# Memory attention woven with a Mixer MLP: when the Mixer's first and last layers may take weight buffers, what margin the planner gives their loads, and which queue carries the final prefetch

## The chip, the cores and the metric

One core of a Trainium2 chip runs the whole kernel as one static program. The metric is device time in microseconds (us), the median of several runs. The mean granted TensorE clock lay between 0.984 and 0.991 of full speed in all of them. The kernel before takes about 3534 us.

## The reference

Two kinds of layer alternate on 2048 tokens of width 640: A, B, A, B, each with its LayerNorm and residual.

```python
# A: recurrent memory attention; 64 segments of 32 tokens, 8 memory tokens carried along
for s in range(n_seg):
    h = jnp.concatenate([mem, xs], axis=1)          # 40 rows
    q, k, v = h @ Wq, h @ Wk, h @ Wv                # 32 heads of 192
    ...                                             # masked softmax, p @ v
    o = jnp.einsum('bhte,hed->btd', o, Wo)
    mem = o[:, :M, :]                               # the next segment needs this
# B: Mixer MLP
h = gelu(layernorm(x) @ w1)
hs = shifted(h) @ w2                                # four quarters, shifted by -1, +1, -2, +2 tokens
x1 = x + hs
return x1 + gelu(layernorm(x1) @ w3) @ w4
```

The recurrence through `mem` forces one attention step after another. The kernel runs the second A layer five steps behind the first, so that 69 steps handle both ("two lanes", 80 columns). A step needs all of Wq, Wk, Wv and Wo. The kernel keeps about three fifths of them on the chip (3 of 5 blocks of each head group's Wq, Wk and Wv); the rest, 48 blocks of Wq, Wk and Wv and 18 of Wo, is streamed again in each step.

## The kernel before

Every instruction is first described to a planner as an operation with an engine, a duration, a due time and the buffers that it touches. A list scheduler then places them: on each engine it takes, among those that can start at once, the one with the earliest due time. What it places is the order of the program. All it believes of transfers are these constants.

```python
HG = 4                       # heads in a group: 8 head groups in a step
RING = 16; RING_A = 14; RING_B = 5    # weight buffers; attention's and Mixer's caps
STEP = 48.0; HOLD = 4.0
W1 = (0.15, 0.04); W2 = (0.4, 0.04); W3 = (0.75, 0.055); W4 = (1.5, 0.025)   # due: first, per block, in steps
LAT = 0.2; DMA_RATE = 345.0e3; DMA_LAT = 2.2; DMA_SKEW = 2.0; FLIGHT = 10
```

```python
    # in Plan.place, when operation o is placed
    if o.dma:
        srv = max(s + DMA_LAT, srv) + o.dma / DMA_RATE
        done = srv + DMA_SKEW
    ...
    for b in o.slots:
        b.left -= 1
        b.free_at = max(b.free_at, done + LAT)      # buffer free again
    ...
    for x in o.succ:
        if o.dma:
            at = done                               # user may start
```

Attention's loads ("ra" buffers) go out from SyncE, Mixer's ("rb") from GpSimd. Each queue is sorted by due time and stays in that order. A load is issued as soon as its buffer is free, however early that is; nothing else holds it back, but for a limit of ten transfers in flight on SyncE (`FLIGHT`). Which buffer a load gets is fixed by the plan.

```python
    def load_b(c, nm, n, due):
        if c >= NCH - 2:
            return ahead[nm, n]                     # last two chunks: prefetched
        b = ring("rb")
        ...
        add("POOL", POOL_US, due, fn, w=(b,), dma=P * wd * 2, queue="wb")

    # attention: the loads of Wo of all eight head groups (held is true for each of them) are due
    # in the last 4 us of the step, those of the last head group's Wv along with its matmuls
    at = base + STEP - HOLD + 0.5 * g if held else s0 + 1.9 * sl
    ws = [block(t, "o", g, c, at + 0.03 * c) for c in range(GC)]

    # last Mixer layer
    def chunk_end(c):
        ...
        for n in range(FC):                         # 12 blocks
            due = D(W4[0] + W4[1] * n)
            wb, wv = load_b(c, "w4", n, due)
            ...                                     # two matmuls of 320 columns: "y"

    # main loop: a chunk per pair of steps
    for t in range(T_A):
        c = (t - 2) // 2 if t >= 2 and t % 2 == 0 else None
        mixer = chunk(c) if c is not None else iter(())
        next(mixer, None)
        attention_step(t)
        for _ in mixer: pass
        if c is not None:
            chunk_end(c)
```

When the weights that stay resident have been used for the last time, `prefetch` loads the 32 weight blocks of the last two chunks into their tiles, from GpSimd (a chunk has w1 5, w2 5, w3 10 and w4 12 blocks).

## Time and profile before

| | before |
|---|---|
| time, median of 3 runs | 3533.37 us (3530.52 to 3536.09) |
| TensorE (PE) busy | 96% of the span |
| PE's stalls over full pace in 28 pairs of steps | 88.5 us |
| DMA | 308 GB/s mean |

Full pace means columns / 2.4 GHz + 2.5 ns for each matmul; the prediction derives it. A stall is a distance between two starts that exceeds this by over 20 ns. The second measure that I use throughout is a place in time: a pair of steps holds 16 head groups, numbered 0 to 15, and "12.05" is 5% into group 12. Groups 7 and 15 end a step, and so does the hand-over of `mem` to the next one.

The same stretch as a window of the profile: the columns are its length, then each engine's busy time and number of instructions, the granted clock, the DMA share and GB/s.

```profile
350.00:3200.00 2850.00, 2797.93 (x69832) 2737.28 (x69829) 2029.09 (x5929) 1456.10 (x2962) 735.56 (x1306) 1.00 0.95 311
```

The first pair after the length is PE. In a kernel whose PE is always busy, the number of matmuls done in a fixed stretch is a better sign of speed than the busy time: 69832 here.

The names in the lines that follow: psk, psq and psv are PE's matmuls for K, Q and V, psy those of attention's output projection (with Wo), y those of the Mixer's last layer (with w4). `wst` is a buffer of the ring, and what follows its arrow is the weight that was loaded into it.

### The profile page before, as it was taken

How to read it: one execution, taken by the hardware profiler on the slowest of the kernel's cores; microseconds unless marked ns; L12 is line 12 of the kernel's file. 1: busy time of each engine (PE TensorE's matmuls, PEld its weight loads, DVE VectorE, ACT ScalarE, POOL GpSimd, SP SyncE). 2: the span in 40 equal slices, each digit the busy share in tenths (PEclk: the TensorE clock that was granted, in tenths of full speed). 3: DMA queues.
4: the chain of work that ended last, by engine and by line, in shares of the span. 5: the costliest groups of instructions: out<-in, count | busy, mean ns of one | idle time of the engine just before them, and what ended most of it. 6: DMA issues, size and time to landing. Idle time of an engine off the chain costs nothing.

```text
span 3534.4 us, 194661 instructions
## 1 busy us (share of the span) xinstructions
PE 3384.3 (96%) x84693; PEld 3257.0 (92%) x84693; DVE 2378.1 (67%) x7184; ACT 1714.3 (49%) x3583; POOL 883.9 (25%) x1581
## 2 busy tenths in 40 slices
PE   6899999999999999999999999999999999999897
PEld 4789999999999999999999999999999999999786
DVE  2456777777666777676677776766667777766455
ACT  2334555545554555454445554545455554554343
POOL 1022222222222222222222222222222222222222
PEclk9999999999999999999999999999999999999898
DMA  9999999999999999999999999999999999999995
GB/s 339 308 304 312 311 314 311 312 309 316 311 314 310 312 309 307 315 304 311 301 314 310 306 315 309 308 305 313 308 310 324 310 313 308 313 309 313 298 317 193
DMA packets 735258, 1089.24 MB, mean 308 GB/s; under 512 B 95358, under 2 KB 691596, under 8 KB 734400
## 3 DMA queue, kind: packets, MB, share of 16 engines
q1 hardware_dynamic: 669504, 874.19, 75.5%
q0 software_dynamic: 64896, 202.59, 17.1%
q8 instruction: 662, 10.85, 1.3%
q14 instruction: 196, 1.61, 0.1%
HBM read 1071.16 MB, written 5.24 MB: 305 GB/s over the span
## 4 chain that ended last, share of the span: by engine, by line
PE 80%; DMA 14%; issue 4%; DVE 1%; POOL 1%; ACT 0%; SPq 0%; POOLq 0%; DVEq 0%; ACTq 0%
PE psy L653 15%; PE psq L514 14%; PE psv L555 14%; PE psk L514 14%; DMA wst<-in_B_w_dram 5%; PE psvt L567 5%; PE pss L586 4%; PE pso L634 4%; PE psh L1025 3%; DMA wst<-in_A_Wv_dram 3%; DMA wst<-in_A_Wo_dram 2%; PE y L1047 2%; PE pst L619 2%; PE hs L994 1%; PE psh L968 1%
## 5 line engine op out<-in xcount | busy, mean ns | idle before, releaser
L472 POOL DMA_DIRECT2D wst<-in_B_w_dram x1056 | 581.7, 551 | 1690.5 <-PE psy L653 387.9
L640 DVE CAST oT<-pso 128x480 bf16<-128x480 f32 (+1 forms) x552 | 342.3, 620 | 413.6 <-PE pso L634 412.6
L571 ACT COPY V<-psvt 80x768 bf16<-80x768 bf16 (+1 forms) x552 | 439.3, 796 | 332.1 <-PE psvt L567 323.5
L514 PEld LDWEIGHTS <-wst 128*128 128x128 bf16 x13248 | 555.6, 100 | 31.2 <-issue 10.2
L653 PE MATMUL psy<-oT,wo 128*128 128x80 bf16 (+1 forms) x10350 | 511.0, 199 | 21.1 <-DMA wo<-in_A_Wo_dram 9.1
L522 ACT CAST qT<-psq 128x480 bf16<-128x480 f32 (+1 forms) x552 | 292.5, 530 | 441.7 <-PE psq L514 364.2
L555 PE MATMUL psv<-hT,wv 128*128 128x80 bf16 (+1 forms) x9936 | 477.8, 199 | 6.2 <-issue 3.5
L514 PE MATMUL psk<-hT,wk 128*128 128x80 bf16 (+1 forms) x9936 | 465.0, 199 | 5.6 <-issue 4.2
L514 PE MATMUL psq<-hT,wq 128*128 128x80 bf16 (+1 forms) x9936 | 454.7, 199 | 12.4 <-DMA wq<-in_A_Wq_dram 7.1
L561 ACT CAST vTs<-psv 128x480 bf16<-128x480 f32 (+1 forms) x552 | 292.1, 529 | 335.0 <-PE psv L555 325.0
L653 PEld LDWEIGHTS <-wo 128*128 128x128 bf16 x10350 | 423.0, 99 | 28.3 <-issue 12.5
L597 DVE CUSTOM_DVE_ANT_1 pss<-pss,mask 80x320 f32<-80x320 f32 (+1 forms) x512 | 245.8, 480 | 270.3 <-PE pss L586 228.5
L555 PEld LDWEIGHTS <-wv 128*128 128x128 bf16 x9936 | 405.3, 99 | 20.2 <-issue 4.3
L514 PEld LDWEIGHTS <-wk 128*128 128x128 bf16 x9936 | 399.7, 100 | 14.4 <-issue 6.5
L514 PEld LDWEIGHTS <-wq 128*128 128x128 bf16 x9936 | 393.6, 100 | 20.8 <-DMA wq<-in_A_Wq_dram 8.1
L514 PE MATMUL psk<-hT,wst 128*128 128x80 bf16 (+1 forms) x6624 | 352.9, 199 | 8.6 <-issue 8.0
L653 PE MATMUL psy<-oT,wst 128*128 128x80 bf16 (+1 forms) x6210 | 351.8, 199 | 8.8 <-DMA wst<-in_A_Wo_dram 4.7
L555 PE MATMUL psv<-hT,wst 128*128 128x80 bf16 (+1 forms) x6624 | 342.6, 199 | 12.4 <-DMA wst<-in_A_Wv_dram 9.2
L624 ACT COPY PT<-pst 80x320 bf16<-80x320 bf16 (+1 forms) x552 | 223.0, 404 | 261.6 <-PE pst L619 258.8
L514 PE MATMUL psq<-hT,wst 128*128 128x80 bf16 (+1 forms) x6624 | 326.2, 199 | 8.3 <-DMA wst<-in_A_Wq_dram 5.2
L604 ACT ACTIVATE pss<-pss,sm 80x320 f32<-80x320 f32 (+1 forms) x552 | 261.4, 474 | 137.4 <-DVE sm L597 137.3
L609 DVE TENSOR_REDUCE sm<-pss 80x4 f32<-80x320 f32 (+1 forms) x552 | 251.9, 456 | 92.5 <-ACT pss L604 91.7
(135 smaller groups left out, 5501.6 us busy)
## 6 DMA issues: line engine op xcount, KB each, us to landing
wst<-in_A_Wk_dram SPq DMA_DIRECT2D x1104, 192.0 KB, 4.7
wst<-in_A_Wq_dram SPq DMA_DIRECT2D x1104, 192.0 KB, 4.7
wst<-in_A_Wv_dram SPq DMA_DIRECT2D x1104, 192.0 KB, 4.8
wst<-in_A_Wo_dram SPq DMA_DIRECT2D x1242, 160.0 KB, 4.7
wst<-in_B_w_dram POOLq DMA_DIRECT2D x726, 160.0 KB, 5.0
wst<-in_B_w_dram POOLq DMA_DIRECT2D x330, 192.0 KB, 5.3
wk<-in_A_Wk_dram SPq DMA_DIRECT2D x8, 576.0 KB, 7.6
wq<-in_A_Wq_dram SPq DMA_DIRECT2D x8, 576.0 KB, 7.4
```

The costliest lines, as they stand in the source:

```text
L472: return (nc.sync if B_SP else nc.gpsimd).dma_start(out=T(b)[:, 0:wd], in_=src)
L514: nc.tensor.matmul(out=o[:, c, 0:N], lhsT=w[:, c * P:(c + 1) * P], rhs=h[:, kc, c0:c0 + N], start=pq.begin(), stop=True, skip_group_check= ...
L522: nc.scalar.copy(out=q[:, :, 0:N], in_=T(pq)[:, :, 0:N])
L555: nc.tensor.matmul(out=o[:, c, 0:N], lhsT=w[:, c * P:(c + 1) * P], rhs=h[:, kc, c0:c0 + N], start=pv.begin(), stop=True, skip_group_check= ...
L561: nc.scalar.copy(out=vs[:, :, 0:N], in_=T(pv)[:, :, 0:N])
L571: nc.scalar.copy(out=V_[0:N, :, 0:Dh], in_=T(pt)[0:N].rearrange("n c f -> n (c f)").rearrange("n (i e) -> n i e", i=HG))
L597: nc.vector.tensor_tensor_reduce(out=o, in0=o, in1=maskt.unsqueeze(1).to_broadcast([N, HG, N]), scale=-scale, scalar=3.0e38, op0=ALU.add, ...
L604: nc.scalar.activation(out=o, in_=o, func=ACT.Exp, bias=sm_[0:N, 0:1], scale=-1.0)
L609: nc.vector.reduce_sum(out=sm_[0:N, 4:4 + HG], in_=o, axis=AX.X)
L624: nc.scalar.copy(out=Pt[0:N, :, 0:N], in_=T(pst)[0:N, :, 0:N])
L640: nc.vector.tensor_copy(out=o_[:, :, 0:N], in_=T(pso)[:, :, 0:N])
L653: nc.tensor.matmul(out=T(psy[j])[:, m - m0, c0:c0 + N], lhsT=w[:, m * P:(m + 1) * P], rhs=o_[:, c, 0:N], start=psy[j].begin(), stop=True, ...
```

## The change

The intent is to leave more of the 16 buffers to attention: the Mixer's weights should sit in them only shortly before use.

1. w1 waits until the last head group of the step before its chunk begins.
2. The twelve w4 blocks wait, four at a time, for head groups 2, 3 and 4 of the chunk's second step (10, 11 and 12 of the pair). For that the description of `chunk_end` moves behind the second step's attention.
3. The planner counts a GpSimd load as ready 1.5 us later, and a Mixer buffer as free 0.5 us after its last use, not 0.2.
4. The final prefetch goes through SyncE's queue, sorted with attention's loads, 8 us later.

The waits of 1 and 2 exist in the plan alone. The planner places such a load after the marked matmul, but no semaphore goes with it; on the chip GpSimd goes on as soon as the former user of the block's buffer is done.

```diff
+B_SLACK = 1.5
+AH = 8.0
+B_FREE = 0.5
...
-                b.free_at = max(b.free_at, done + LAT)
+                b.free_at = max(b.free_at, done + (B_FREE if b.cls == "rb" else LAT))
...
-                    at = done
+                    at = done + (B_SLACK if o.e == "POOL" else 0.0)
...
-    def load_b(c, nm, n, due):
+    def load_b(c, nm, n, due, after=()):
...
+                mark[t, g] = now[:1]          # first Q matmul of head group g of step t
...
-                return nc.gpsimd.dma_start(out=tl[:, i % 3, 0:wd], in_=src)
-            add("POOL", POOL_US, base + at * 0.6 * STEP, fn, ..., queue="wb")
+                return nc.sync.dma_start(out=tl[:, i % 3, 0:wd], in_=src)
+            add("SP", SP_US, base + at * 0.6 * STEP + AH, fn, ..., queue="wa")
...
-            wb, wv = load_b(c, "w1", kc, due)
+            wb, wv = load_b(c, "w1", kc, due, mark.get((2 * c + 1, NG - 1), ()))
...
-            wb, wv = load_b(c, "w4", n, due)
+            wb, wv = load_b(c, "w4", n, due, mark.get((2 * c + 3, 2 + n // 4), ()))
...
-        if c is not None:
-            chunk_end(c)
+        if t >= 3 and t % 2 == 1:
+            chunk_end((t - 3) // 2)
```

(Comments are mine, and long lines are cut at "...".)

More of the change, by code (lines that the diff above doesn't have):

```diff
@@ L472, in fn @@
             return (nc.sync if B_SP else nc.gpsimd).dma_start(out=T(b)[:, 0:wd], in_=src)
-        add("SP" if B_SP else "POOL", SP_US if B_SP else POOL_US, due, fn, w=(b,), dma=P * wd * 2, queue="wb")
+        add("SP" if B_SP else "POOL", SP_US if B_SP else POOL_US, due, fn, w=(b,), dma=P * wd * 2, queue="wb", after=after)
         return b, lambda: T(b)[:, 0:wd]
@@ L485 @@
     last = [()]
+    mark = {}
     def HX(t, kc):
@@ L848, in fn @@
             def fn(op, tl=tl, i=i, wd=wd, src=src):
-                return nc.gpsimd.dma_start(out=tl[:, i % 3, 0:wd], in_=src)
-            add("POOL", POOL_US, base + at * 0.6 * STEP, fn, w=(ub,), a=(b,), dma=P * wd * 2, queue="wb")
+                return nc.sync.dma_start(out=tl[:, i % 3, 0:wd], in_=src)
+            add("SP", SP_US, base + at * 0.6 * STEP + AH, fn, w=(ub,), a=(b,), dma=P * wd * 2, queue="wa")
             ahead[nm, n] = ub, lambda tl=tl, i=i, wd=wd: tl[:, i % 3, 0:wd]
@@ L1123 @@
             pass
-        if c is not None:
-            chunk_end(c)
-    for c in range((T_A - 2 + 1) // 2, NCH):
-        for _ in chunk(c):
-            pass
-        chunk_end(c)
+        if t >= 3 and t % 2 == 1:
+            chunk_end((t - 3) // 2)
+    chunk_end(NCH - 2)
+    for _ in chunk(NCH - 1):
+        pass
+    chunk_end(NCH - 1)
     placed = plan.place()
```

## The prediction

> **What bounds the kernel now.** The kernel is one static order of instructions that a planner inside it lays out. 69 attention steps (8 head groups each) stream their weights through a ring of 16 buffers; a Mixer chunk is woven into each pair of steps, and its 32 weight blocks (w1: 5, w2: 5, w3: 10, w4: 12) go through the same ring, at most 5 buffers at a time, issued by GpSimd. I read the page first: engine shares, slices, queues.
>
> ```profile
> PE 3384.3 (96%) x84693; PEld 3257.0 (92%) x84693; DVE 2378.1 (67%) x7184; ACT 1714.3 (49%) x3583; POOL 883.9 (25%) x1581
> ...
> PE   6899999999999999999999999999999999999897
> ...
> GB/s 339 308 304 312 311 314 311 312 309 316 311 314 310 312 309 307 315 304 311 301 314 310 306 315 309 308 305 313 308 310 324 310 313 308 313 309 313 298 317 193
> ```
>
> TensorE is nearly full from 350 to 3200 us, DMA moves about 311 GB/s all along. A 96% busy PE may still hide slack, so I took the distance between starts of matmuls from the trace. In one piece of the timeline 18 K/Q/V matmuls of 80 columns take 0.81 us, the last one modelled as 0.20: 0.61 / 17 = 36 ns each, which is 80 / 2.4 GHz + 2.5 ns. If every matmul between 350 and 3200 us took only columns (at least 64) / 2.4 GHz + 2.5 ns, they would need 2747 of the 2850 us. So the middle of the run is PE-bound to 96.4%, and the most that any better ordering of loads can win there is 103 us. Of the 103, I counted gaps of over 20 ns by what ended them: 42 us nothing that the profile shows ("issue"), 35 us a weight DMA, 12 us VectorE; the rest is spread thinly.
>
> Then the waits of PE:
>
> ```profile
> engine line waited for: us in total, times, longest us
> PE y L1047 <- DMA wst<-in_B_w_dram: 14.6, 23, 1.9
> PE psv L739 <- DVE vb L731: 13.8, 7, 3.9
> PE psk L514 <- issue: 12.2, 14, 2.4
> ...
> PE psv L555 <- DMA wst<-in_A_Wv_dram: 9.2, 13, 2.3
> ...
> PE psq L514 <- DMA wst<-in_A_Wq_dram: 5.2, 6, 1.3
> PE psy L653 <- DMA wst<-in_A_Wo_dram: 4.7, 10, 1.1
> ```
>
> The largest single wait is "y", the Mixer's last layer, for its own weights w4. To place the stalls I numbered the head groups of a pair of steps 0 to 15 (28 pairs, steps 8 to 63, 100.1 us each) and summed PE's excess by group: group 7 28 us, groups 13 and 14 together 22.5 us (of which y on w4 20.9), group 15 15 us, everything else 23 us. So the w4 stall costs 0.75 us per chunk.
>
> Last, why w4 is late, from GpSimd's timeline around one chunk:
>
> ```profile
> 1020.23 1.19 POOL L472 DMA_DIRECT2D wst<-in_B_w_dram  x2 [1.23 <-DMA wst<-in_A_Wq_dram]
> 1022.00 0.55 POOL L472 DMA_DIRECT2D wst<-in_B_w_dram  x1 [0.58 <-PE y L1047]
> 1024.58 0.55 POOL L472 DMA_DIRECT2D wst<-in_B_w_dram  x1 [2.03 <-PE psq L514]
> ...
> 1028.61 0.60 POOL L472 DMA_DIRECT2D wst<-in_B_w_dram  x1 [1.40 <-PE psv L555]
> ...
> 1053.46 0.59 POOL L472 DMA_DIRECT2D wst<-in_B_w_dram  x1 [3.54 <-PE pss L586]
> ```
>
> These first five are w1 of the next chunk; its first matmul starts at 1052.71, so five of sixteen buffers are taken for 26 to 32 us. Over all chunks the medians are: w1 is issued in groups 14.0 to 15.3 and used in group 2.7 of the next pair. w4 blocks 0 to 4 are issued in groups 8.0 to 10.1 and wait 5 to 11 us landed; blocks 5 to 11 must wait for those buffers, are issued from 12.05 on, fly about 5 us, and reach PE 0.0 to 0.8 us ahead of use, in each case with some chunks at zero. The planner believes that they come in time; they do not. All Mixer blocks together hold 446 buffer-us per pair, 28% of the ring's 1600.
>
> **What the Trainium skill says.** "TensorE: Matmul & The Clock Gate", section "Wait — 56ns, not 53.3ns?", gives N / 2.4 GHz + about 2.5 ns for warm back-to-back matmuls; the 36 ns above agrees, and my floor rests on it. "Perfetto Trace Analysis", "Identifying the Most-Contended Engine", warns that matmul busy share does not show the distance to the roofline; here it said 98% in the middle where the floor says 96.4%, so both leave little. "DMA: Bandwidth & Descriptors", "Issuing engines are not separate DMA queues": loads from different engines share the same 16 DMA engines, so moving the final prefetch from GpSimd to SyncE should buy no bandwidth, only an order. The trace can't quite confirm it: the fastest stretch of the end, 3465 to 3470 us, ran at 376 GB/s with both queues active.
>
> **The change, part by part.** No byte, matmul or vector instruction is added or removed; only order, waits and buffers.
>
> (1) w1 waits for the first Q matmul of group 7 of the step before its chunk (15.0 on my scale). Medians were 13.97, 14.13, 14.46, 15.00, 15.25, so three blocks move by about 1.1, 0.9 and 0.6 groups. At some 4.5 us a group: 12 buffer-us freed per pair. w1 stays over 20 us early, so nothing is risked.
>
> (2) w4 blocks 0-3, 4-7, 8-11 wait for groups 10, 11, 12 of the pair. Blocks 0 to 4 move from 8.0, 9.1, 9.4, 9.7, 10.1 to 10.2 (11.2 for block 4), some 25 buffer-us. Blocks 5 to 11 are issued after 12.05 already, so the marks do not bind them. Together with (1) 37 buffer-us, 37 / (1600 - 446) = 3% more ring for attention, all in groups 8 to 11 and 13 to 15.
>
> (3) The planner now takes a GpSimd load as ready 1.5 us later and a Mixer buffer as free 0.5 us (not 0.2) after use. w4 landed 0 to 0.8 us ahead at the median and the longest wait was 1.9; with 1.5 us more nearly all those waits vanish, since PE has K/Q/V work of later groups to put in between. I take 85% of 0.75 us x 34 chunks = 25.5: 22 us.
>
> (4) Attention's weight waits on PE between 350 and 3200 us are what remains of the 35 us after y's 20.9: 14 us. More ring in groups 13 to 15, where a third of them are (group 15 had 4.2 on Wo and 1.6 on Wv), saves perhaps 5 us.
>
> (5) The first and last five steps have one lane, thus matmuls of 40 columns; there PE is about 91% busy by the modelled ends and the loads set the pace at 301 to 315 GB/s. 3% more ring there is worth at most 3% of some 450 us; since up to ten transfers are in flight whatever the ring holds, I take a quarter to a third, 4 us.
>
> (6) The last chunks' 32 blocks now go by SyncE in one queue with step 68's weights, 8 us later. Before, GpSimd threw them in between and three times PE stood still for 0.8 to 2.3 us on Wv and Wq. But all the same bytes must land before the second-last chunk's y, and then the last chunk's chain follows (from 3504 to 3534 us, unchanged). 0 to 5 us; I take 2.
>
> Sum: 22 + 5 + 4 + 2 = 33 us. 3533 - 33 = 3500.
>
> **Rivals.** (a) The wait only moves: w4 pushed against its use by the marks makes all twelve blocks just-in-time, where five were safe. For: a 5 us flight, and a mark at 10.2 that lands block 0 at about 11.3, where its use was at 11.5. Against: the 1.5 us margin is known to the planner, which then uses y later, and y has no deadline before group 16. If it holds, the y stall stays and the time is within 0.3%: 3525 to 3540. (b) PE is bound by things that loads do not touch: 42 us "issue", 12 us VectorE. That is certain and caps the gain at about 103 us for a perfect order; it makes over 2% (71 us) unlikely. (c) The freed ring does more than I give it: DMA reached 340 to 354 GB/s in groups 9 and 10, where the ring refills, against 296 to 310 in groups 7, 13 to 15. If attention runs further ahead, part of group 7's 28 us and group 15's 15 us goes too: 3465 to 3480. (d) One ordered queue for the end makes SyncE the bottleneck or lets w4 arrive after attention is done: 5 to 10 us lost at the end.
>
> **Range and chances.** Any change of the plan shuffles the whole static order; I allow 10 us for it either way on top of (a) and (c). Range 3468 to 3527. Over 2% faster needs 3463: nearly all weight waits and half of "issue" gone, 9%. Over 2% slower needs 71 us of new stalls, and the marks leave slack everywhere but at w4: 2%.
>
> **What would show it.** Right: PE's wait "y for wst from B_w" falls from 14.6 to under 4 us; w1's issue bunches after the start of group 7; between 350 and 3200 us the work that was done there takes about 25 us less; the final chain from psx to the output store still takes 30 us. Wrong: y's wait is as large as before or comes back as attention waiting for Wk, Wq, Wv (rival a); "issue" grows as the loads run denser; the last step lengthens beyond its 59 us.

## The result and the profile after

| | before | after |
|---|---|---|
| median of 4 runs | 3534.73 us (3530.52 to 3537.48) | 3549.91 us (3542.94 to 3554.97) |
| ratio of the means | | 1.0043, 95% interval 1.0021 to 1.0064 |
| needed at full pace by the matmuls between 350 and 3200 us | 2747 us | 2738 us |
| stalls of PE in 28 pairs | 88.5 us | 93.7 us |

A ratio is the mean time of one kernel's fast runs over that of the other's of the same rounds, so it is not quite the ratio of the medians that stand beside it. The change made the kernel 0.4% slower, where 0.9% faster was predicted; 3549.91 lies above the range of 3468 to 3527.

The page of the changed kernel, engine shares and slices:

```profile
PE 3393.7 (96%) x84693; PEld 3263.4 (92%) x84693; DVE 2366.3 (67%) x7184; ACT 1716.2 (48%) x3583; POOL 840.6 (24%) x1549
...
GB/s 339 316 308 302 309 306 311 306 307 311 308 312 312 309 306 315 295 314 313 309 309 307 295 302 317 309 315 315 313 315 306 317 310 316 309 316 317 306 297 172
```

Nothing in these lines tells which kernel is slower: the same matmuls, the same 96%, the same rate. The window from 350 to 3200 us tells it:

```profile
350.00:3200.00 2850.00, 2793.11 (x69574) 2733.13 (x69572) 2013.89 (x5917) 1455.01 (x2954) 711.57 (x1304) 1.00 0.95 310
```

PE issued 258 matmuls fewer than before in the same 2850 us. PE's waits, with the same columns as in the prediction:

```profile
PE psv L560 <- DMA wst<-in_A_Wv_dram: 27.7, 39, 2.1
PE psv L744 <- DVE vb L736: 13.0, 5, 4.3
PE psy L658 <- DMA wst<-in_A_Wo_dram: 9.9, 21, 1.9
...
PE y L1052 <- DMA wk<-in_B_w_dram: 1.7, 2, 1.0
```

The wait of y for w4 in the ring, the largest before, is gone from the list altogether; what y still waits for, 2.0 us in all, are blocks of the final prefetch (`wk` and `wv` are resident tiles that it fills). In place of the old wait PE waits 27.7 us, not 9.2, for streamed blocks of Wv, and 9.9, not 4.7, for streamed Wo. The sum of those two grew by 23.7 us, more than the 14.6 that went.

GpSimd's timeline around the last layer of one chunk (the one just before the w1 loads that the prediction's timeline shows):

```profile
1007.91 0.54 POOL L475 DMA_DIRECT2D wst<-in_B_w_dram  x1 [21.54 <-DMA wst<-in_A_Wq_dram]
1008.99 0.54 POOL L475 DMA_DIRECT2D wst<-in_B_w_dram  x1 [0.54 <-PE psq L518]
...
1014.54 0.56 POOL L475 DMA_DIRECT2D wst<-in_B_w_dram  x1 [2.09 <-PE psv L560]
1016.39 0.54 POOL L475 DMA_DIRECT2D wst<-in_B_w_dram  x1 [1.29 <-PE y L1052]
...
1033.23 0.54 POOL L475 DMA_DIRECT2D wst<-in_B_w_dram  x1 [5.12 <-DMA wst<-in_A_Wo_dram]
```

GpSimd stands for 21.5 us, until head group 10, and issues w4 blocks 0 and 1. Block 2 goes out 5.6 us after block 1: in between GpSimd issues small loads for the next chunk (cut here), then it waits 2.1 us for a matmul with Wv, the last user of the buffer that the plan has given to block 2. Counted from issue to last use, 10 to 12 of the 16 buffers are attention's at that time and 2 the Mixer's, so some stand empty. The last line is the first block of the next chunk's w1, at 15.21 on the scale of groups; before it was at 13.97, the 1020.23 of the prediction's lines (at this point the trace of the changed kernel is 7 us behind). Over 28 pairs the median issue of w4 moved from 8.01, 9.09, 9.42, 9.71, 10.12, 12.05 ... 13.67 to 10.45, 10.74, 12.04, 12.24, 12.41, 12.74 ... 14.30, and the last y from 14.80 to 15.25.

The time that the change adds to the run can be split along the trace, with a caution that follows. In the two profiled runs, of 3534.4 and 3551.0 us, the second-last attention step starts 4.0 us later, lasts 6.0 us longer (45.9 and 51.9), the last step and the chain to the output store add 0.2, and from the issue of the last store to the end of the program it takes 6.4 us longer (3.5 and 9.8). The 4.0 is the sum of 1.2 us before step 8, 5.6 us in the 28 pairs (100.34 instead of 100.14 us each) and 2.9 us won back in steps 64 to 66. The caution: one profile is one execution. The changed kernel, the one with the old prefetch and the one with half of it (both below) run the same instructions on PE in the same order up to step 64; their profiles reach that step 4.5 and 11.8 us apart from the changed kernel's, with stalls of 93.7, 91.3 and 88.3 us. So of this split only the last part is firm; it comes back in every run with the new prefetch. GpSimd's last line of before and of after, in the timeline (start, length, what it does):

```profile
3530.95 0.58 POOL L1065 DMA_DIRECT2D out_dram<-xo  x1 [11.36 <-DVE xo L1053]
```

```profile
3541.17 0.56 POOL L1070 DMA_DIRECT2D out_dram<-xo  x1 [11.36 <-DVE xo L1058]
```

The store lands 1.8 us after its issue in both. Along with its issue starts a DRAIN of GpSimd, an instruction of the kernel's end that the timeline does not list; the program's last instructions wait for it. The trace records 2.72 us for it before and 9.07 after.

### The profile page after: what moved, and what is told of

It reads as the page before. It is cut to its first block, busy times and chain, and to the rows that moved or that the text cites. A ratio compares the mean times of both kernels' runs of the same rounds, so it can differ in the third digit from the quotient of the medians.

```text
span 3551.0 us, 194390 instructions
## 1 busy us (share of the span) xinstructions
PE 3393.7 (96%) x84693; PEld 3263.4 (92%) x84693; DVE 2366.3 (67%) x7184; ACT 1716.2 (48%) x3583; POOL 840.6 (24%) x1549
## 5 line engine op out<-in xcount | busy, mean ns | idle before, releaser
L475 POOL DMA_DIRECT2D wst<-in_B_w_dram x1056 | 572.9, 543 | 2148.1 <-DMA wst<-in_A_Wq_dram 431.6
L658 PE MATMUL psy<-oT,wo 128*128 128x80 bf16 (+1 forms) x10350 | 520.3, 199 | 15.2 <-DMA wo<-in_A_Wo_dram 7.8
L518 PE MATMUL psk<-hT,wk 128*128 128x80 bf16 (+1 forms) x9936 | 491.0, 199 | 7.4 <-issue 5.5
L518 PEld LDWEIGHTS <-wk 128*128 128x128 bf16 x9936 | 413.6, 100 | 18.3 <-issue 7.4
L560 PE MATMUL psv<-hT,wst 128*128 128x80 bf16 (+1 forms) x6624 | 352.1, 199 | 29.7 <-DMA wst<-in_A_Wv_dram 27.7
L518 PE MATMUL psq<-hT,wst 128*128 128x80 bf16 (+1 forms) x6624 | 343.3, 199 | 9.4 <-DMA wst<-in_A_Wq_dram 4.2
L535 DVE CAST kT<-psk 128x320 bf16<-128x320 f32 (+1 forms) x552 | 253.6, 459 | 102.5 <-PE psk L518 102.0
```

Of the source, the lines that this page charges most:

```text
L475: return (nc.sync if B_SP else nc.gpsimd).dma_start(out=T(b)[:, 0:wd], in_=src)
L518: nc.tensor.matmul(out=o[:, c, 0:N], lhsT=w[:, c * P:(c + 1) * P], rhs=h[:, kc, c0:c0 + N], start=pq.begin(), stop=True, skip_group_check= ...
L535: nc.vector.tensor_copy(out=k4[:, :, 0::3, 0:N], in_=p4[:, :, 0::2, 0:N])
L560: nc.tensor.matmul(out=o[:, c, 0:N], lhsT=w[:, c * P:(c + 1) * P], rhs=h[:, kc, c0:c0 + N], start=pv.begin(), stop=True, skip_group_check= ...
L658: nc.tensor.matmul(out=T(psy[j])[:, m - m0, c0:c0 + N], lhsT=w[:, m * P:(m + 1) * P], rhs=o_[:, c, 0:N], start=psy[j].begin(), stop=True, ...
```

## The experiments

First I had four theories, by the four parts. A: w1's blocks, held back to group 15, bunch there and collide with the loads at the step's end. B: w4 is too late, and its loads crowd out attention's. C: the margins only move PE's wait from w4 to attention's weights. D: the loss lies in the end of the program, from the new prefetch. Each of the first four kernels is the changed kernel with one part undone. (All four undone give the order of before, instruction by instruction.) Unless a run says otherwise, "measured" is the median of six fast runs, with the ratio to the kernel before of the same rounds on the same chip and its 95% interval; a point is a hundredth of that ratio, 35 us; the "middle" is 350 to 3200 us of the profiled run.

**w1's wait undone.**

```diff
-load_b(c, "w1", kc, due, mark.get((2 * c + 1, NG - 1), ()))
+load_b(c, "w1", kc, due)
```

> The changed kernel with the wait of w1 alone taken out. Theory A (bunching): the wait lets all five w1 loads go together in group 15 (issued at 15.2 to 15.7), in the middle of the stream of Wo and Wv, and this delays Wv of group 15 (18.0 us of waits in 28 pairs) and Wk and Wq of group 0 (7.8 us). Then without it PE's wait for streamed Wv falls from 27.7 us to about 10, and the time from about 3548 to about 3527. Theory B (late w4): the wait of w4 is to blame, and here the Wv wait stays above 20 us and the time at 3543 to 3553. Theory D (the end): the same as B, and the last two steps stay as they are.

Measured: 3547.68 us, 1.0039 (1.0018 to 1.0060), the same as the changed kernel. A falls. The stalls of group 15 even rose, from 23.4 to 43.7 us in 28 pairs, 19.2 of them waits of Wo's matmuls for attention's own output `oT` from VectorE, while groups 0 and 7 lost less. Here w4 blocks 2 and 3 go out at 11.05 and 11.31 (12.04 and 12.24 in the changed kernel) and block 11 at 13.90 (14.30), and the time is the same. So the slow order has more than one form, and the wait for Wv is only one of them.

**w4's wait undone.**

```diff
-load_b(c, "w4", n, due, mark.get((2 * c + 3, 2 + n // 4), ()))
+load_b(c, "w4", n, due)
```

> The changed kernel with the wait of w4 alone taken out. Theory B (late w4): the wait gives w4's buffers to attention, w4 gets them back only after group 12, the last y falls to group 15.25 and the buffers that w1 needs come free late, so all runs together in group 15. Then without it the last y is back at about 14.8, PE's wait for streamed Wv falls from 27.7 to about 10 us, and the time to about 3527. Theory A (bunching of w1): Wv waits stay above 20 us, time 3543 to 3553. In both the y wait stays under 4 us, if the margin is what removed it; if the wait of w4 removed it, it is back at some 15 us.

Measured: 3506.92 us, 0.9924 (0.9903 to 0.9944). This one wait costs 1.19 points against the changed kernel, 42 us. B is right as to the part. The waits of PE:

```profile
PE psv L560 <- DMA wst<-in_A_Wv_dram: 17.5, 19, 2.4
...
PE y L1052 <- DMA wst<-in_B_w_dram: 0.7, 2, 0.4
```

y still hardly waits, and PE did more:

```profile
350.00:3200.00 2850.00, 2810.91 (x70392) 2756.07 (x70389) 2041.87 (x5981) 1471.53 (x2988) 734.26 (x1317) 1.00 0.95 313
```

That is 818 matmuls more than the changed kernel and 560 more than before. Stalls in 28 pairs fell from 93.7 to 62.5 us. The last y is at 15.13, hardly earlier than 15.25 and not back at 14.8 as B expected, so a late y alone is not the explanation. Nor did the wait for Wv fall to 10 us: by what ended them, the 31 us of stalls that w4's wait adds in 28 pairs are 13 us for Wv, 5 for Wq and Wk and 10 for which the profile shows no cause ("issue").

**The margins undone.**

```diff
-B_SLACK = 1.5
+B_SLACK = 0.0
-B_FREE = 0.5
+B_FREE = 0.2
```

> The changed kernel with the margins set back (0 and 0.2 us instead of 1.5 and 0.5). If the margin is what removed the waits of y for w4, they are back, at 14 us or more (with the wait of w4 all twelve blocks come just in time, so up to 25 us). Theory C (the margins only move the wait on: PE takes attention work in y's place and runs into weights that are not there): the wait for streamed Wv falls from 27.7 to about 12 us and the sum of both stays within 8 us of now, time within 6 us of the changed kernel. Theories A and B: Wv waits stay, y waits come on top, time 3560 to 3570.

Measured: 3539.05 us, 1.0002 (0.9979 to 1.0025). In the waits, y is back and Wv is gone:

```profile
PE y L1052 <- DMA wst<-in_B_w_dram: 17.2, 30, 1.5
...
PE psv L560 <- DMA wst<-in_A_Wv_dram: 4.8, 10, 1.0
```

Beside w4's wait the margins bring nothing, and what they take from y turns up at Wv: C describes the waits of this pair of kernels. In time, undoing the margins even gains 0.4 points, uncertain by 0.3, where C had expected the same within 6 us. It is not the whole story, as the next kernel but one shows.

**The old prefetch.**

```diff
-nc.sync.dma_start(...);   add("SP", ..., base + at * 0.6 * STEP + AH, ..., queue="wa")
+nc.gpsimd.dma_start(...); add("POOL", ..., base + at * 0.6 * STEP, ..., queue="wb")
```

> The changed kernel with the last chunks' weights fetched as before (from GpSimd, 8 us earlier). Theory D (the end): in the two profiles the start of step 67 was only 4.0 us later after the change and the end 16.6 us later, of which 6.5 us are a longer drain of GpSimd after the last store (9.1 us instead of 2.7). If the new prefetch makes that, the drain is back at about 3 us and the time 6 to 12 us shorter, 3537 to 3542. If the end is noise of the static order, or the drain varies by itself, the time stays within 4 us.

Measured: 3535.80 us, 1.0000 (0.9982 to 1.0018). The new prefetch costs some 0.4 points, with an uncertainty of about 0.3; the last DRAIN of GpSimd is back at 2.70 us, which is 6.4 of it. D holds, for a smaller part of the loss than w4's wait.

The next questions were what the parts are worth without w4's wait, and whether the ring is really what attention lacks. Theory E: attention takes the buffers that w4 leaves and holds them; they do not make it faster, and w4 can't get them back in time. Theory F: transfers are merely moved from groups 8 to 10, where the queues had room, to the end of the pair, where they are dense.

**Margins alone.**

```diff
 # the kernel before, plus
+B_SLACK = 1.5
+B_FREE = 0.5
```

> The kernel before with the two margins alone (a GpSimd load counts as ready 1.5 us later, a Mixer buffer as free after 0.5 us); no waits for w1 and w4, the old prefetch, the old place of the last layer in the program. If the margins are the whole gain that was seen without the wait of w4 (3507 with the new prefetch, whose end was some 9 us longer), this is at 3493 to 3503, with y's waits for w4 under 3 us. If the gain there needed the wait of w1, it is at 3515 or more.

Measured: 3517.64 us, 0.9939 (0.9919 to 0.9959). The margins are worth 0.61 points, 21.5 us of some 3535. Stalls in 28 pairs fell from 88.5 to 70.7; 17.8 x 34 / 28 = 21.6 us for all 34 pairs of steps, the same. The wait of y is 0.2 us, and the stalls of groups 13 and 14 fell from 22.5 to 0.8 us. If the margins were all, 3493 to 3503 was expected; so they are not.

**Margins and w1's wait.** This is the changed kernel without w4's wait and with the old prefetch.

```diff
-load_b(c, "w4", n, due, mark.get((2 * c + 3, 2 + n // 4), ()))
+load_b(c, "w4", n, due)
 # and the old prefetch as above
```

> The changed kernel without the wait of w4 and with the old prefetch: what is left are the wait of w1 and the margins. If the two losses simply add (40 us for the wait of w4, 6.3 us of GpSimd's drain and up to 6 us more for the new prefetch), the time is 3493 to 3501 and the last drain 2.7 us. If the new prefetch costs nothing but the drain, 3500. A time within 3 us of the kernel with the margins alone says that the wait of w1 does nothing.

Measured: 3504.79 us, 0.9902 (0.9885 to 0.9919). Against the margins alone, on the same chip in the same rounds, that is 13 us better, give or take 9. The two kernels also differ in where `chunk_end` is described, so the 13 us belong to both together. Wv's wait is 9.4 us. The two losses added up would have left 3493 to 3501; it is a few us more.

**Eleven buffers for attention, with the whole change.**

```diff
-RING_A = 14
+RING_A = 11
```

> The changed kernel with attention held to 11 of the 16 buffers, so that five stay for the Mixer and w4 gets its buffers as soon as its wait lets it. Theory E (buffers): the wait of w4 hurts because attention takes w4's buffers and does not give them back before group 12; then here w4 blocks 2 to 4 are issued at 10.7 to 11.3 instead of 12.0 to 12.4, the Wv wait of 27.7 us halves, and the time falls below 3530. Theory F (transfers): the wait hurts because it moves the transfers of w4 from groups 8 to 10, where the DMA engines have room, to groups 11 to 15, where they are full; buffers are not what attention lacks. Then the time stays at 3540 to 3560 although w4 has its buffers.

Measured: 3537.47 us, 1.0001 (0.9983 to 1.0018): three buffers fewer, and 0.4 points faster than the changed kernel. Its waits:

```profile
PE psy L658 <- DVE oT L645: 14.7, 33, 0.6
...
PE psv L560 <- DMA wst<-in_A_Wv_dram: 4.9, 10, 1.4
```

w4 blocks 2 to 4 are now issued at 10.63, 11.40 and 12.07 instead of 12.04 to 12.41, and Wv's wait is down from 27.7 to 4.9 us. In its place stands the wait for `oT`. E is half right: the freed buffers gave attention nothing, and taking them did harm; but giving them back does not bring the 42 us.

**Eleven buffers, without w4's wait.**

```diff
-RING_A = 14
+RING_A = 11
-load_b(c, "w4", n, due, mark.get((2 * c + 3, 2 + n // 4), ()))
+load_b(c, "w4", n, due)
```

> The changed kernel without the wait of w4, and attention held to 11 buffers instead of 14. Theory E (buffers): three buffers fewer for attention cost it time: 3525 or more, against 3507 with 14. Theory F (transfers): attention does not use more than 11 to gain time, since its transfers in flight stayed at 6.0 to 6.5 in groups 8 to 10 whether w4 held buffers there or not: 3500 to 3515.

Measured: 3518.48 us, 0.9943 (0.9927 to 0.9959). With the run before, this makes a square: w4's wait costs 1.19 points with 14 buffers and 0.58 with 11, and three buffers fewer cost 0.2 points where the wait is absent. So about half of the wait's cost goes through attention's cap of 14 buffers, 0.6 points with an uncertainty of 0.4. The time lies between what E (3525 or more) and F (3500 to 3515) expected.

For the rest there were two ideas. Theory G: the Mixer's last layer itself comes later in the pair, and that costs. Theory H: at the end of a step Wv of the last head group is in the queue behind Wo, and it comes late whenever the other loads are pushed there. To test G without any wait added, the next three kernels start from the margins with w1's wait, 0.9902.

**Last layer due earlier, and later.**

```diff
-W4 = (1.5, 0.025)
+W4 = (1.375, 0.025)    # earlier; (1.625, 0.025) for later
```

> The best so far (wait of w1, margins, old prefetch, no wait of w4; 3505 us) with the last layer due one head group earlier (1.375 steps instead of 1.5). Theory G (late y): what remains of the loss by the wait of w4, when buffers are taken out of it, is that y falls into group 15, where the last head group's chain (the copy of oT by VectorE before the last output projections) is then uncovered. Then an earlier y gains or keeps: 3495 to 3505, with the last y before group 15 and the wait for Wv in group 15 (9.3 us in 28 pairs) smaller. If y's place does not matter, 3505 within 4 us. If earlier y only meets its weights too early, waits of y for w4 come back, 5 us or more.

> The same with the last layer due one head group later (1.625 steps), with no wait on its loads. Theory G (late y): y alone, moved late without any wait on its loads, costs: 3520 to 3540, with 10 us or more of stalls added in group 15 of the 28 pairs. If it is only the loads that matter (theories E and F), they can go as early as before, and the time stays at 3500 to 3510.

Measured: 3511.45 us, 0.9943 (0.9922 to 0.9963) earlier, and 3545.34 us, 1.0027 (1.0008 to 1.0047) later. The last layer due an eighth of a step later, with no wait on loads added, costs 1.25 points: the last y moves to 15.41, and stalls in 28 pairs rise from 63.0 to 94.8 us. But this does not part y from its loads. A load's due time is that of its matmul; the first w4 block is still issued at 7.93, but blocks 6 to 11 go out at 13.42 to 15.06 instead of 12.26 to 13.66. Nor are the stalls where G has them: group 15 takes 6 of the added 32 us, group 9 takes 13. So it is shown that a late last layer with its loads can cost this much, and not that a late y alone does. In the kernel without w4's wait the last y is at 15.13 and in the slow one at 15.25, which is a small step for it. Earlier tests nothing of G: the last y stayed at 15.14, and the first moved from 11.53 to 11.48. That it lost time, with a wait for Wv of 14.3 us, is open.

**A larger margin.**

```diff
-B_SLACK = 1.5
+B_SLACK = 2.5
```

> The best so far with 2.5 us instead of 1.5 us of margin for GpSimd's loads. y's waits for w4 are already under 1 us at 1.5, so a larger margin has nothing left to remove at y; w3 and w2 have margins of their own. Expected 3500 to 3515, the same as with 1.5, or worse by up to 10 us if a later y costs (theory G).

Measured: 3550.19 us, 1.0044 (1.0018 to 1.0070), as slow as the changed kernel, with w4's loads at their old place (7.93 to 13.95). Its largest wait is that of the changed kernel, PE for Wv, with 27.2 us in 41 times. The last y is at 15.22. So F, taken as "the transfers of w4 moved", is not needed for the slow order: one more microsecond of believed latency gives as slow a kernel.

**Half of the prefetch by SyncE.** The first 20 blocks go by SyncE, the last 12 (w4) by GpSimd, in the changed kernel.

```diff
+            sp = i < 20          # SyncE with AH for these, GpSimd as before for the rest
```

> The changed kernel with 20 of the last chunks' 32 blocks fetched by SyncE and the 12 of the last layer by GpSimd, one look for the end alone. GpSimd's drain after the last store was 2.7 us in all three profiles with the old prefetch and 9.0 to 9.1 us in all five with the new one. If the drain depends on whether GpSimd issued transfers within some 60 us of the end, it is back at 2.7; if it depends on the number that GpSimd issued in all, it may be anything between; if it depends on the prefetch being on SyncE at all, 9.

One look, one run, its state unknown: 3537.97 us, beside 3532.48 us for the kernel before. The last DRAIN took 10.05 us; the time itself says nothing, for the reason given above. That GpSimd still has loads to issue near the end does not bring the short DRAIN back; its cause stays open.

**Wv first.** In the changed kernel the loads of the last head group's Wv are due 2 us earlier; nothing else is edited.

```diff
-wb, wv = block(t, "v", g, kc, due)
+wb, wv = block(t, "v", g, kc, due - (2.0 if g == NG - 1 else 0.0))   # the load; the matmul keeps its due time
```

> The changed kernel with one more edit: the loads of Wv for the last head group of a step are due 2 us earlier, so that they stand before all of Wo in SyncE's queue instead of between the tenth and the eleventh block. Theory H (late Wv): the wait of w4 lengthened the transfers at the step's end (5.8 us in group 7 and 4.9 in group 15 for Wv, against 4.8 and 4.3 before), and Wv, issued last and used first, is what they hit; then the wait for streamed Wv falls from 27.7 us to under 5, and the time by 20 us or more, from 3550 to 3530. Rival (the plan is longer in itself, and PE would stand still elsewhere): the Wv wait falls, but Wo, Wk or Wq waits grow by as much, and the time stays within 6 us of 3550.

Measured: 3524.44 us, 0.9965 (0.9950 to 0.9980): a gain of 0.78 points, about 27 us, on the changed kernel with w4's wait in it. SyncE's timeline at the end of a step, in the changed kernel and then here:

```profile
1077.59 7.79 SPq L451 DMA_DIRECT2D wst<-in_A_Wo_dram  x10
1085.49 1.92 SPq L451 DMA_DIRECT2D wst<-in_A_Wv_dram  x2
1087.50 4.79 SPq L451 DMA_DIRECT2D wst<-in_A_Wo_dram  x8
```

```profile
1070.18 4.14 SPq L451 DMA_DIRECT2D wst<-in_A_Wv_dram  x4
1074.41 13.16 SPq L451 DMA_DIRECT2D wst<-in_A_Wo_dram  x18
```

The two blocks of Wv no longer stand behind ten of Wo, which take 7.8 us to issue because each waits for a buffer. They land 6.7 us (group 7) and 4.0 us (group 15) ahead of use at the median, where it was 0.2 and 0.1. The waits of PE:

```profile
PE psy L658 <- DMA wst<-in_A_Wo_dram: 18.1, 28, 2.1
...
PE psv L560 <- DMA wst<-in_A_Wv_dram: 4.8, 7, 1.4
```

Wv's wait fell by 22.9 us and Wo's rose by 8.2. In 28 pairs the stalls fell from 93.7 to 73.0 us, by 9.6 in group 7 and 12.3 in group 15, where H has them. The edit also reshuffled w4: blocks 2 and 3 go out at 11.06 and 11.29, a group earlier than in the changed kernel. But they did so in the run without w1's wait too, which was slow, so the gain is hardly theirs. H is the largest single cause found: 27 us of the 42, give or take 9, come back without touching w4's wait.

**The best of both.** Margins, w1's wait, no w4 wait, the old prefetch, and Wv first.

```diff
 # margins and w1's wait as above (0.9902), plus
+wb, wv = block(t, "v", g, kc, due - (2.0 if g == NG - 1 else 0.0))
```

> The best so far (wait of w1, margins, old prefetch, no wait of w4; 3500 to 3505 us) with the same edit. Theory H: its Wv wait of 9.4 us falls to under 4, 3492 to 3500. Rival: within 4 us, or slower because Wo comes 1 us later.

Measured: 3498.38 us, median of four fast runs (3496.83 to 3500.96), 0.9893 (0.9873 to 0.9913). It beats both kernels by 1.1% and 1.5%. Stalls in 28 pairs are 55.4 us, the fewest of all, and the wait for Wv is 1.1 us. Against 0.9902 without the Wv line, on another chip, the intervals overlap: the line is worth much where loads crowd the step's end and little where they don't. Seen the other way, w4's wait costs 1.0 to 1.2 points with the old order of Wv. With Wv first the two kernels lie 0.72 points apart, of which the new prefetch has 0.2 to 0.4, so that the wait costs 0.3 to 0.5, uncertain by 0.4.

## Why the prediction was wrong, point by point

In order, the parts add up like this, each kernel's ratio to before in points of a hundredth, 1 point being 35 us; stalls are those of 28 pairs:

| kernel | ratio | step of time | stalls |
|---|---|---|---|
| before | 1 | | 88.5 |
| + margins | 0.9939 | -21.5 us | 70.7 |
| + w1's wait | 0.9902 | -13 us | 63.0 |
| + w4's wait | 1.0000 | +35 us | 91.3 |
| + new prefetch: the change | 1.0043 | +15 us | 93.7 |

Each step is a difference of two ratios, thus uncertain by some 9 us. The steps of the stalls, times 34 / 28, are -21.6, -9.3, +34.4 and +2.9: for the first three they are the same story read from the trace; the last is within what two profiles of one order differ by.

**What bounds the kernel, right.** PE needs 2747 of 2850 us at full pace, and even the best kernel here, with 2780, stays inside that frame. The time was lost and won within 103 us, as said.

**Step (3), the margins, right by themselves.** 22 us predicted, 21.5 measured when they are added alone, by the mechanism named: y's wait goes to 0.2 us. (The 34 chunks of the sum are 33; the last two of the 35 are prefetched.) The prediction then added this to steps that it took for independent. They are not: within the whole change the margins bring nothing (1.0002 without them, 1.0043 with them).

**Step (1), w1's wait, too small.** Its 12 of the 37 freed buffer-us make it a third of the 5 us of step (4), under 2 us; it measured 13 us, of which some may be `chunk_end`'s. With w4's wait present it is worth nothing (1.0039 without it, 1.0043 with it).

**Steps (2) and (4), w4's wait, the step that failed.** "Blocks 5 to 11 are issued after 12.05 already, so the marks do not bind them", and more ring "saves perhaps 5 us": in truth the wait costs 35 us, or 42 measured from the changed kernel. Three things in that step were wrong.

- The marks do bind blocks 5 to 11, through the ring. In the kernel before, w4's first five blocks hold their buffers from group 8 on, and blocks 5 to 11 inherit them. Held back, they lose the buffers to attention in the plan (which gives it 13.9 of its 14 in group 10, 10.9 before), and the queue, which is in order, goes on only as PE frees others: 12.74 instead of 12.05 for block 5, 14.30 instead of 13.67 for block 11. I had read the issue times of the kernel before as if they were fixed. This delay is not by itself what costs: without w1's wait it was half as long or less, 12.39 and 13.90, and the kernel was as slow.
- Attention did not lack buffers in groups 8 to 10. The change freed more than the 37 buffer-us of the prediction: counted from issue to last use, the Mixer's blocks held 450 buffer-us per pair before and 378 after. Attention had 10.0, 10.6 and 10.8 buffers in use in these groups before and 9.8, 10.1 and 11.7 after, so most of what was freed stood empty. SyncE had 5.7 to 6.3 transfers in flight there before and 6.0 to 6.5 after, and what the DMA engines moved in groups 9 and 10 fell from 339 and 354 to 309 and 310 GB/s, while group 12 rose to 350 and group 15 from 296 to 320. With 11 buffers instead of 14 the changed kernel became faster.
- I took no account of who waits at the end of a step. 18 blocks of Wo and the last two of Wv are issued there, and Wv is used at once. Its slack was 1.6 us (group 7) and 0.7 us (group 15) before. With w4 among them it became 0.2 and 0.1. This is the second half of my rival (a), "comes back as attention waiting for Wk, Wq, Wv", which I had dismissed because the planner knows of its margin for y. It has none for SyncE's loads, which it believes to land on time. Bringing Wv forward gives 27 us back.

What is shown: that w4's wait is the part to blame, that about half its cost needs the cap of 14 buffers, and that putting Wv before Wo gives back more than half of it. These overlap and are not to be added. A late Wv is not the only form of the loss: without w1's wait its slack was 0.9 and 0.3 us, better than in the kernel with the margins alone (0.7 and 0.3), and the kernel was slow, waiting for `oT` and Wo. One microsecond more margin, or the last layer an eighth of a step later, gives a kernel about as slow in other ways again.

What in the planner tips the order is not shown, but one part can be read without the chip, by running the planner of each kernel and taking the length that it believes in. That is 3388.9 us without w4's wait and 3403.1 with it, both with the old prefetch (3504.8 and 3535.8 measured). So a plan that is longer even with every load on time may be some 14 of the 35 us. That is an estimate and no more, since over all these kernels the believed length does not follow the measured time (3439.7 with eleven buffers, for 3537.5). For the changed kernel it is 3402.8 us, and 3404.3 with Wv first (3549.9 and 3524.4 measured): the gain of Wv first is none that the planner sees, which fits loads that come later than it believes.

**Step (5), the one-lane steps, not tested apart.** No run isolates it, and single profiles are too uneven for it: the 1.2 us lost before step 8 and the 2.9 us won in steps 64 to 66 are less than two profiles of one and the same order can differ by (7.8 us at step 8, for the two kernels without w4's wait).

**Step (6), the prefetch, wrong in sign.** +2 us gained was predicted; it costs 15 us in the sequence above, give or take 10, or 8 if taken without w4's wait (0.9924 and 0.9902, intervals overlapping). Of that, 6.4 us are GpSimd's last DRAIN, 9.07 instead of 2.72 us, which nothing in the profile of before announced: all kernels with the full prefetch on SyncE show 8.99 to 9.07, all with it on GpSimd 2.67 to 2.73. Rival (d) saw a loss of 5 to 10 us at the end, for another reason; there is something of it too, as SyncE issues w4 of the last chunks only after the 18 Wo, from 3502.7 to 3509.4 us, when attention itself ends at 3509.5, and y waits 2.0 us for them:

```profile
3497.46 5.17 SPq L451 DMA_DIRECT2D wst<-in_A_Wo_dram  x8
3502.68 0.42 SPq L854 DMA_DIRECT2D wk<-in_B_w_dram  x1
3503.15 2.41 SPq L854 DMA_DIRECT2D wq<-in_B_w_dram  x3
```

The chain from the last layer's psx to the output store, though, is unchanged (26.8 and 27.3 us), as predicted.

**The range.** 10 us for the reshuffled order was too little: single edits of one constant moved the time by 1.25 and 1.42 points, 44 and 50 us. And rival (a) was priced at "the y stall stays", 3525 to 3540; it did not stay, it moved to a place where it cost more.

## What to carry to other kernels

A buffer kept from one stream is not yet one that another can use; ask what the first will find when it comes back, and whether the other had lacked buffers at all, which its transfers in flight tell. A load should be delayed only if the place it moves to has slack; here the end of a step had the least, 0.7 to 1.6 us for Wv. In a shared in-order queue, put what is used first before what is used next: that edit of one line gave back 27 us where the buffer policy had cost 42, and nothing measurable where the policy was absent. And gains that are each right alone need not add up in one static order: the margins were worth 21 us alone and nothing beside w4's wait.

## What the Trainium skill lacked or had wrong

- "VectorE: DVE Perf Modes", section "The DRAIN you can't avoid", tells of two kinds of DRAIN: VectorE's own after each operation, and those of preamble and postamble, about 12 ns each on all five engines. The one met here is neither. GpSimd's DRAIN at the end of the kernel took 2.67 to 2.73 us in kernels whose final prefetch GpSimd issued, 8.99 to 9.07 where SyncE issued all of it and 10.05 where they shared it. It lies on the path to the end. I found no page that says what sets it, and no run here shows it.
- "DMA: Bandwidth & Descriptors", section "Anatomy of one DMA — SWDGE (gpsimd) path", fits one transfer as 2.0 us + bytes / 436e3. For GpSimd's w4 blocks of 160 KB that would be an estimated 2.4 us; with the queues full at 310 GB/s the median from issue to landing was 5.0 us before and 4.9 after. A planner for a loaded chip needs the second figure.
- "Perfetto Trace Analysis", section "Optimization Strategy", says that a gap that keeps recurring can mean too few buffers. Here the gap at Wv recurred (39 times, 27.7 us) with 14 buffers and fell to 4.9 us with 11: so it was not a lack of buffers, and bringing Wv forward in the queue took it away too (4.8 us). I found no page that treats two streams on one ring of buffers.
